# A planned one-core kernel: same-engine delays and shaken orders in its planner, a third bank for its second layer, and one engine of forty of its steps changed

## The chip, the cores and the metric

The kernel runs on one core of a Trainium2 chip. The metric is the device time of one execution in microseconds (us). The kernel before was run three times: 559.52, 560.00 and 560.67 us, median 560.0.

The core has TensorE (PE in the profile, its weight loads PEld), VectorE (DVE), ScalarE (ACT), GpSimd (POOL) and SyncE (SP), which issues all transfers here. Each engine works through its own list of instructions in order and waits on semaphores for the others. TensorE writes its results to eight banks of PSUM; this kernel calls them S0 to S3, Y0, Y1, G and D.

## The reference

Three parts follow one another; the output of one is the input of the next.

```
y   = attention with decay over x, a, B, C        # 4 x 8 heads, 768 positions
h   = max(y @ w1, y @ w2, y @ w3)                 # 3072 tokens, 256 -> 768
x2  = h @ w_out                                   # 768 -> 256
t   = x2 @ w_in                                   # 256 -> 2048
P   = a0 + a1 t + a2 t^2 + a3 t^3
Q   = 1 + |b0| |t| + |b1| t^2
out = (P / (Q + 1e-6)) @ w_out2                   # 2048 -> 256
```

## The kernel before

The 3072 tokens are worked on in six groups of 512. For each group there is an attention part, a first layer ("g": 18 tiles of the three products with their maximum, then 2 "y" tiles with w_out) and a second layer of 16 steps. Values are split into a high and a low part, and each product is three matmuls, high by high, high by low and low by high, made by `mm3`:

```
    pe.matmul(dst, wh, hi, start=first, stop=False)
    pe.matmul(dst, wh, lo, start=False, stop=False)
    pe.matmul(dst, wl, hi, start=False, stop=last)
```

In the trace these are L845, L846 and L847. Step s of the second layer (`h_plan`, s from 0 to 95) makes one tile t of 128 x 512 with six of them ("h matmuls", weights win) in a PSUM bank, S0 or S1. ScalarE, GpSimd and VectorE then compute the rational function from t in a chain of some ten operations, and the last two make its high part (ScalarE, L366) and low part (GpSimd, L1073). `o_plan` adds the step's share of the output with six more matmuls ("o matmuls", the step's A tiles by the weights in L, into S2 and S3). The first layer's tiles of the next groups go to the banks G and D; after each of its products ScalarE copies the bank (L366) or VectorE takes the maximum with it (L935).

There are several ways to compute the rational function, called kinds. HV gives the kinds of the steps of groups 0 to 4 in turn, HL those of group 5. In kind H, ScalarE makes two values from t (L1042 and L1044), GpSimd one linear expression and one product (L1028, L1046), and VectorE multiplies twice with the bank t as an operand (L1047, L1048). L1048 is the last reader of the bank. Kind J differs from H in one operation: the linear expression is made by ScalarE (L1025). Kind A uses a square on ScalarE (L1051) and ends its use of the bank with L1058. All kinds end in a logarithm and an exponential on ScalarE (L1060, L1061) and three VectorE operations (L1062, L1065, L1067), each with one operand in a Y bank and one in SBUF.

The order of all this is not written out by hand. Every piece of work is handed to `Plan.op` with its engine, an assumed cost, what it reads and writes, and the banks or buffers it may use; `Plan.emit` then tries 8 rounds of 6 list schedules, each with latest start times from the best one so far, keeps the one with the earliest end, and emits the instructions in its order. So one constant can change the order on all engines.

Of the kernel before, what the change touches and what calls it, by code (L numbers as in the profile page):

```python
# [3 lines left out]

# [7 lines left out]
F32 = mybir.dt.float32  # L12
# [3 lines left out]
AF = mybir.ActivationFunctionType  # L16
ALU = mybir.AluOpType
# [16 lines left out]
OL = 6  # L34
SBANKS, DBANKS, FIRST_BANKS, GBANKS = (), ("D", "G"), ("G", "D", "S0", "S1", "S2", "S3"), ("G", "D")
LAST, LAST_R = ("G", "D", "S0", "S1"), ("Y0", "Y1")
HV, HL = "JAJH", "HHKK"
EARLY, SPILL = (0, 1, 2), (1, 2)
WARM = 9
PIECE = 2.6  # L40
# [7 lines left out]
class _Tile:  # L48


    def __init__(self, make=None, places=(), kind=None):
        self.make, self.places, self.t, self.place, self.kind = make, places, None, None, kind or places
        self.first, self.writers, self.readers = None, [], []


class _Op:

    def __init__(self, i, engine, busy, fn, first, deps, after, at, lock, mode, size):  # L60
        self.i, self.engine, self.busy, self.fn, self.first = i, engine, busy, fn, first
        self.deps, self.after, self.at = deps, after, at
        self.lock, self.mode, self.size = lock, mode, size
        self.plain = busy + (Plan.SWITCH if mode else 0.0)
        if engine == "dma":
            self.busy = busy + 0.06
            self.moves = 0.14 + size / 350.0 if size > 30.0 else 0.08
            self.plain = max(self.busy, self.moves)
        self.uses = [engine, "pool"] if lock else [engine]

    def lag(self, then):
        if self.engine == "dma":
            return Plan.FIRST_BYTE + self.moves + Plan.LANDED
        if self.engine == then.engine:
            return self.plain
        return self.plain + Plan.TAIL[self.engine] + (0.05 if then.engine == "pool" else 0.0)


# [19 lines left out]
class Plan:  # L98
# [3 lines left out]

    TAIL = {"pe": 0.22, "act": 0.15, "dve": 0.135, "pool": 0.09}
    SWITCH, FIRST_BYTE, LANDED, FLIGHTS, BEGIN = 0.12, 1.25, 1.35, 8, 0.65
    ROUNDS, LOOK, KEEP = 8, (0.0, 0.1, 0.2), (0.0, 1.5)

    def __init__(self):
        self.ops, self.fixed, self.tiles, self.turns = [], {}, [], {}
# [7 lines left out]
        return t  # L116

    def op(self, engine, busy, fn, reads=(), writes=(), at=None, behind=(), lock=False, mode="", size=0.0,
           turn=None):


        i = len(self.ops)
        deps, after = set(), {w for t in behind for w in t.writers}
        for k in [turn] * bool(turn) + [t.kind for t in writes if t.first is None and len(t.places) > 1]:
            if k in self.turns:
                after.add(self.turns[k])
            self.turns[k] = i
        for t in reads:
            assert t.writers
            deps.update(t.writers)  # L130
            t.readers.append(i)
        for t in writes:
            if t.first is None:
                t.first = i
                for p in getattr(t, "prevs", ()):
# [5 lines left out]
        self.ops.append(_Op(i, engine, busy, fn, [t for t in writes if t.first == i and t.places], deps,  # L141
                            after - deps, at, lock, mode, size))

    def listed(self, key, look, keep):

# [10 lines left out]
        place, had = {}, {}  # L156

        def behind(js, i, t):
            e = ops[i].engine
            for j in js:  # L160
                if ops[j].engine == e != "dma":
                    t = max(t, start[j] + ops[j].busy)
                else:
                    t = max(t, end[j] + (0.05 if e == "pool" else 0.0))
            return t
# [113 lines left out]
    def emit(self):  # L279

        ops, n = self.ops, len(self.ops)
        self.before, self.then, self.touch = [[] for _ in range(n)], [[] for _ in range(n)], [[] for _ in range(n)]
        for o in ops:
            for i in o.deps | o.after:
                l = 0.0 if i in o.after else ops[i].lag(o)
                self.before[o.i].append((i, l))
                self.then[i].append((o.i, l))
        self.of_fixed, self.open_fixed = {}, {}
        for p, ts in self.fixed.items():
            self.of_fixed[p] = [i for t in ts for i in t.writers + t.readers]  # L290
            self.open_fixed[p] = 0
            for t in ts:
                t.place = p
                self.open_fixed[p] += len(set(t.writers + t.readers))
        for t in self.tiles + [t for ts in self.fixed.values() for t in ts]:
            for i in set(t.writers + t.readers):
                self.touch[i].append(t)
        span = [o.plain for o in ops]
        key = [0.0] * n
        for i in reversed(range(n)):  # L300
            key[i] = min([1e9 if ops[i].at is None else ops[i].at] + [key[j] - l for j, l in self.then[i]])
        best = None
        for _ in range(self.ROUNDS):
            for look in self.LOOK:
                for keep in self.KEEP:
                    order, start, end, had = self.listed(key, look, keep)
                    if best is None or end < best[0]:
                        best = end, order, start, had, self.place
            start, had = best[2:4]
            before, then = [list(b) for b in self.before], [list(b) for b in self.then]  # L310
            for j, js in had.items():
                for i in js:
                    l = ops[i].lag(ops[j])
                    before[j].append((i, l))
                    then[i].append((j, l))
            back = [[(j, l - span[i] + span[j]) for j, l in then[i]] for i in range(n)]
            mirror = self.placed([-(start[i] + span[i]) for i in range(n)], back, before)
            far = max(mirror[i] + span[i] for i in range(n))
            key = [far - mirror[i] - span[i] for i in range(n)]
        start = best[2]  # L320
        for i in best[1]:
            for t in ops[i].first:
                t.t = t.make(best[4][t])
            ops[i].fn()
# [3 lines left out]
def decay_attention_max_moe_rational_moe(  # L328
# [49 lines left out]
    def plan_conv(tok, nm, src, k0, c0):  # L378
# [39 lines left out]

        for k in range(2):
            op("pool", 0.7, lambda k=k: pool.tensor_tensor(  # L420
                out=a.t[:, k], in0=a.t[:, k], in1=e.t[:, k], op=ALU.add), [e], [a])
        op("act", 0.54, lambda: copy(act, hi(), af()), [a], [tok])
        for k in range(2):
            op("pool", 0.7, lambda k=k: pool.tensor_tensor(
                out=lo()[:, k], in0=af()[:, k], in1=hi()[:, k].bitcast(F32), op=ALU.subtract), [a], [tok])

    for nm in ("w1", "w2", "w3"):
        w_alloc(nm, KD, DF1)
# [10 lines left out]
    def bank(*places, kind=None):  # L439
        return plan.tile(places, lambda p: ps.tile([128, T], F32, tag=p, name=p), kind=kind)  # L440
# [397 lines left out]
    def c(i):  # L838
        return co[:, i:i + 1]
# [148 lines left out]
    def h_plan(s, c0=0, n=T):  # L988
# [1 line left out]

        last = g == NG - 1
        half = n < T
        t = bank(*(LAST if last else ("S0", "S1")))
        x = n / T

        def f(z):
            return z.t[:, 0:n] if half else z.t

        def aop(cost, fn, reads, writes):
            op("act", cost - 0.43 * (1 - x), fn, reads, writes)  # L1000
# [19 lines left out]
        else:  # L1020
            v, w, t1 = v_r(), w_r(), t1_r()
        r = bank(*(LAST_R if last else ("Y0", "Y1")))
        def linear():
            if kind == "J":
                aop(0.69, lambda: act.activation(out=f(t1), in_=f(v), func=AF.Identity, scale=c(5), bias=c(4)),  # L1025
                    [v], [t1])
            else:
                pop(0.74, lambda: pool.tensor_scalar(out=f(t1), in0=f(v), scalar1=c(5), scalar2=c(4),  # L1028
                                                     op0=ALU.mult, op1=ALU.add), [v], [t1])

        if kind == "K":
            aop(0.5, lambda: copy(act, f(t1), f(t)), [t], [t1])
            aop(0.69, lambda: act.activation(out=f(w), in_=f(t), func=AF.Identity, scale=c(3), bias=c(2)),
                [t], [w])
            pop(1.26, lambda: pool.tensor_tensor(out=f(w), in0=f(t1), in1=f(w), op=ALU.mult), [t1], [w])
            aop(0.5, lambda: act.activation(out=f(v), in_=f(t), func=AF.Abs), [t], [v])
            linear()
            pop(1.26, lambda: pool.tensor_tensor(out=f(v), in0=f(t1), in1=f(v), op=ALU.mult), [t1], [v])
            dop(0.67, lambda: dve.scalar_tensor_tensor(out=f(w), in0=f(w), scalar=c(1), in1=f(t),
                                                       op0=ALU.add, op1=ALU.mult), [t], [w])  # L1040
        elif kind in "HJ":
            aop(0.69, lambda: act.activation(out=f(w), in_=f(t), func=AF.Identity, scale=c(3), bias=c(2)),  # L1042
                [t], [w])
            aop(0.5, lambda: act.activation(out=f(v), in_=f(t), func=AF.Abs), [t], [v])  # L1044
            linear()
# [154 lines left out]
```

## Time and profile before

| | |
|---|---|
| median of three runs | 560.0 us |
| profiled execution, its own time | 562.15 us |
| its span, first to last instruction | 560.2 us |
| mean granted TensorE clock | 0.994 |
| bytes moved | 36.92 MB |

The span is that of the profiled execution; the 1.95 us between it and the execution's own time lie around the program. The profile counts a matmul as busy from its start to its modelled end, so that neighbours overlap: TensorE can look busy while it starts fewer matmuls than it could. The count of matmuls in a stretch is therefore read beside the busy time.

### The profile page before, as it was taken

Reading aid. Unit: us, or ns where it says so; the run is one execution under the profiler, and the core shown is the slowest. Engines: PE = TensorE matmul, PEld = TensorE weight load, DVE = VectorE, ACT = ScalarE, POOL = GpSimd, SP = SyncE. Lnnn points to the kernel's source line nnn. Section 1 sums busy time; section 2 is a strip of 40 time slices with the busy share of each in tenths; the row PEclk is TensorE's granted clock in tenths of the full one; section 3 lists DMA queues with packets and bytes.
Section 4 is the critical chain, followed back from the end, with each engine's and each line's share of the span. In section 5 each row is a group of like instructions: output and inputs, shape, how many; then the busy total and the mean of one; then the engine's idle time right before and its main releaser. Section 6 shows DMA issues by size and latency. Waiting matters only on the chain. (4 is left out here: it accounts for less than half of the span.)

```text
span 560.2 us, 8435 instructions
## 1 busy us (share of the span) xinstructions
PE 541.8 (97%) x2854; PEld 410.8 (73%) x2854; DVE 491.2 (88%) x760; ACT 471.3 (84%) x805; POOL 410.7 (73%) x384
## 2 busy tenths in 40 slices
PE   8899999999999999999899999999999999999996
PEld 3466667888887877777677787777878777876663
DVE  6989999777985789899888898898999889899996
ACT  6989886757776799889798898998989988999883
POOL 1457875788896668767657776786689978779984
PEclk9979999999999999999999999999999999999999
DMA  7667963423702100010300100001000010001001
GB/s 205 240 220 242 328 212 127 139 75 115 261 2 75 39 1 1 0 39 1 113 0 0 39 1 1 1 1 37 2 1 1 0 39 1 1 1 37 1 0 38
DMA packets 15830, 36.92 MB, mean 66 GB/s; under 512 B 2947, under 2 KB 3883, under 8 KB 15787
## 3 DMA queue, kind: packets, MB, share of 16 engines
q1 hardware_dynamic: 15787, 36.38, 19.3%
q8 instruction: 22, 0.36, 0.3%
q14 instruction: 21, 0.17, 0.1%
HBM read 28.89 MB, written 7.49 MB: 65 GB/s over the span
## 5 line engine op out<-in xcount | busy, mean ns | idle before, releaser
L1073 POOL TENSOR_TENSOR A<-A,A 128x512 fp32r<-128x512 f32 x80 | 104.1, 1302 | 40.7 <-ACT A L366 35.5
L1046 POOL TENSOR_TENSOR A<-A,A 128x512 f32<-128x512 f32 x64 | 82.8, 1297 | 10.3 <-ACT A L1025 7.9
L1062 DVE SCALAR_TENSOR_TENSOR A<-A,Y 128x512 f32<-128x512 f32 (+1 forms) x89 | 60.4, 679 | 19.2 <-ACT Y L1061 18.3
L1060 ACT ACTIVATE Y<-A,qc 128x512 f32<-128x512 f32 (+1 forms) x89 | 61.1, 687 | 14.8 <-POOL A L1046 13.7
L420 POOL TENSOR_TENSOR C<-C,E 128x256 uint32<-128x256 uint32 x56 | 44.0, 799 | 34.3 <-DVE C L415 30.7
L1065 DVE SCALAR_TENSOR_TENSOR Y<-A,co,Y 128x512 f32<-128x512 f32 (+1 forms) x89 | 66.5, 747 | 0.3
L846 PE MATMUL S<-A,L 128*128 128x512 f32 x160 | 62.8, 392 | 1.0 <-POOL A L1073 1.0
L1067 DVE SCALAR_TENSOR_TENSOR A<-A,Y 128x512 f32<-128x512 f32 (+1 forms) x89 | 60.8, 683 | 2.9
L845 PE MATMUL S<-A,L 128*128 128x512 f32 x160 | 62.3, 390 | 0.0
L847 PE MATMUL S<-A,L 128*128 128x512 f32 x160 | 62.3, 390 | 0.0
L366 ACT ACTIVATE A<-A 128x512 fp32r<-128x512 f32 x80 | 50.1, 628 | 10.7 <-DVE A L1067 8.9
L1061 ACT ACTIVATE Y<-Y 128x512 f32<-128x512 f32 (+1 forms) x97 | 56.1, 578 | 2.5
L1042 ACT ACTIVATE A<-S,co 128x512 f32<-128x512 f32 x62 | 47.7, 770 | 3.1 <-POOL A L1073 1.7
L1048 DVE SCALAR_TENSOR_TENSOR A<-A,co,S 128x512 f32<-128x512 f32 x62 | 46.3, 747 | 2.0
L1047 DVE TENSOR_TENSOR A<-S,A 128x512 f32<-128x512 f32 x62 | 42.5, 686 | 6.1 <-ACT A L1042 4.3
L463 POOL TENSOR_TENSOR H<-X,H 128x512 fp32r<-128x512 f32 x30 | 40.2, 1339 | 8.7 <-ACT H L366 8.5
L1057 POOL TENSOR_TENSOR A<-A,A 128x512 f32<-128x512 f32 x20 | 25.9, 1296 | 20.6 <-DVE A L1053 16.9
L1044 ACT ACTIVATE A<-S 128x512 f32<-128x512 f32 x62 | 36.7, 592 | 4.3 <-PE S L847 2.4
L845 PE MATMUL S<-K,win_hi 128*128 128x512 f32 (+1 forms) x80 | 33.6, 420 | 3.2 <-DVE A L1048 2.5
L846 PEld LDWEIGHTS S<-A,L 128*128 128x128 f32 x160 | 30.0, 188 | 9.1 <-POOL A L1073 2.7
L845 PEld LDWEIGHTS S<-A,L 128*128 128x128 f32 x160 | 30.0, 188 | 6.4
L847 PEld LDWEIGHTS S<-A,L 128*128 128x128 f32 x160 | 30.0, 188 | 6.1
(214 smaller groups left out, 1613.3 us busy)
## 6 DMA issues: line engine op xcount, KB each, us to landing
R<-in_wo_dram SPq DMA_DIRECT2D x11, 512.0 KB
R<-in_w_dram SPq DMA_DIRECT2D x9, 512.0 KB
R<-in_win_dram SPq DMA_DIRECT2D x8, 512.0 KB
L<-in_xn_dram SPq DMA_DIRECT2D x6, 512.0 KB
out_dram<-A SPq DMA_DIRECT2D x12, 256.0 KB
xt_d<-L SPq DMA_DIRECT2D x4, 512.0 KB
L<-xt_d SPq DMA_DIRECT2D x4, 512.0 KB
y_d<-A SPq DMA_DIRECT2D x8, 256.0 KB
```

Of the source, the lines that this page charges most:

```text
L366: act.activation(out=o, in_=i, func=AF.Copy)
L845: pe.matmul(dst, wh, hi, start=first, stop=False)
L846: pe.matmul(dst, wh, lo, start=False, stop=False)
L847: pe.matmul(dst, wl, hi, start=False, stop=last)
L1042: aop(0.69, lambda: act.activation(out=f(w), in_=f(t), func=AF.Identity, scale=c(3), bias=c(2)), [t], [w])
L1046: pop(1.26, lambda: pool.tensor_tensor(out=f(v), in0=f(t1), in1=f(v), op=ALU.mult), [t1], [v])
L1060: aop(0.6, lambda: act.activation(out=f(r), in_=f(v), func=AF.Ln, bias=qc), [v], [r])
L1061: aop(0.49, lambda: act.activation(out=f(r), in_=f(r), func=AF.Exp, scale=-1.0), [], [r])
L1062: dop(0.6, lambda: dve.scalar_tensor_tensor(out=f(v), in0=f(v), scalar=QC, in1=f(r), op0=ALU.add, op1=ALU.mult), [r], [v])
L1065: dop(0.67, lambda: dve.scalar_tensor_tensor(out=f(r), in0=f(w), scalar=c(0), in1=f(r), op0=ALU.add, op1=ALU.mult), [w], [r])
L1067: dop(0.6, lambda: dve.scalar_tensor_tensor(out=f(w), in0=f(v), scalar=2.0, in1=f(r), op0=ALU.subtract, op1=ALU.mult), [v, r], [w])
L1073: pop(1.26, lambda: pool.tensor_tensor(out=f(lo), in0=f(w), in1=f(hi).bitcast(F32), op=ALU.subtract), [w, hi], [lo])
```

## The change

Four things change.

1. The planner counts 0.12 us (`DRAIN`) between two operations of the same engine (not TensorE, not transfers) when the second uses a tile that the first wrote.
2. After its 8 rounds the planner tries 150 more orders. Each takes the latest start times of the best order so far, shakes those in a randomly drawn stretch by a random amount, and is kept if its planned end is earlier. The draws have a fixed seed.
3. A second-layer step of groups 0 to 4 may use bank D as well as S0 and S1.
4. HV goes from JAJH to HAHH: in groups 0 to 4, 40 steps of kind J become kind H. Kind J is removed from the code.

No instruction is added or removed apart from the 40 that change engine; everything may move.

```diff
-HV, HL = "JAJH", "HHKK"
+HV, HL = "HAHH", "HHKK"
...
         if self.engine == then.engine:
-            return self.plain
+            return self.plain + (Plan.DRAIN if self.i in then.results else 0.0)
...
+    DRAIN = 0.12
-    ROUNDS, LOOK, KEEP = 8, (0.0, 0.1, 0.2), (0.0, 1.5)
+    ROUNDS, SHAKES, LOOK, KEEP = 8, 150, (0.0, 0.1, 0.2), (0.0, 1.5)
...
+        for t in (*reads, *writes):
+            if engine not in ("pe", "dma") and not apart:
+                results.update(w for w in t.writers if self.ops[w].engine == engine)
...
+        draw = random.Random(1)
+        for _ in range(self.SHAKES):
+            key = latest() if draw.random() < 0.3 else best[5]
+            at, reach, by = draw.uniform(0.0, 200.0), draw.choice((10.0, 25.0, 60.0, 600.0)), draw.choice((0.2, 0.6, 1.5))
+            key = [k + (draw.gauss(0.0, by) if abs(k - at) < reach else 0.0) for k in key]
+            attempt(key, draw.choice(self.LOOK), draw.choice(self.KEEP))
...
-        t = bank(*(LAST if last else ("S0", "S1")))
+        t = bank(*(LAST if last else ("S0", "S1", "D")))
...
-        def linear():
-            if kind == "J":
-                aop(0.69, lambda: act.activation(out=f(t1), in_=f(v), func=AF.Identity, scale=c(5), bias=c(4)),
-                    [v], [t1])
...
-            linear()
+            pop(0.74, lambda: pool.tensor_scalar(out=f(t1), in0=f(v), scalar1=c(5), scalar2=c(4),
+                                                 op0=ALU.mult, op1=ALU.add), [v], [t1])
```

The order of the instructions moves on every engine. Two places on TensorE and one on GpSimd show how. A name like S0_4371 is tile 4371 in bank S0; with win it is a second-layer step, with w1, w2 or w3 a first-layer tile, and with L1 an output share. In the changed file mm3's lines are L866 to L868, and L1028, L1046, L1057 and L1073 are L1059, L1061, L1072 and L1088.

TensorE before, steps 53 and 54 of the second layer, near the end of group 3:

```order
L845 MATMUL S0_4371<-K0_3237,win_hi_90 128x512
L846 MATMUL S0_4371<-K1_3252,win_hi_90 128x512
L847 MATMUL S0_4371<-K0_3237,win_lo_91 128x512
L845 MATMUL S0_4371<-K2_3359,win_hi_90 128x512
L846 MATMUL S0_4371<-K3_3407,win_hi_90 128x512
L847 MATMUL S0_4371<-K2_3359,win_lo_91 128x512
L845 MATMUL S1_4383<-K0_3237,win_hi_90 128x512
L846 MATMUL S1_4383<-K1_3252,win_hi_90 128x512
L847 MATMUL S1_4383<-K0_3237,win_lo_91 128x512
L845 MATMUL S1_4383<-K2_3359,win_hi_90 128x512
L846 MATMUL S1_4383<-K3_3407,win_hi_90 128x512
L847 MATMUL S1_4383<-K2_3359,win_lo_91 128x512
```

TensorE in the changed kernel, step 52 and what follows it:

```order
L866 MATMUL D_4215<-K0_3336,win_hi_90 128x512
L867 MATMUL D_4215<-K1_3356,win_hi_90 128x512
L868 MATMUL D_4215<-K0_3336,win_lo_91 128x512
L866 MATMUL D_4215<-K2_3415,win_hi_90 128x512
L867 MATMUL D_4215<-K3_3421,win_hi_90 128x512
L868 MATMUL D_4215<-K2_3415,win_lo_91 128x512
L866 MATMUL G_4229<-xhi0_3283,w2_hi_84 128x512
L867 MATMUL G_4229<-xlo0_3294,w2_hi_84 128x512
L868 MATMUL G_4229<-xhi0_3283,w2_lo_85 128x512
L866 MATMUL G_4229<-xhi1_3322,w2_hi_84 128x512
L867 MATMUL G_4229<-xlo1_3346,w2_hi_84 128x512
L868 MATMUL G_4229<-xhi1_3322,w2_lo_85 128x512
```

Before, steps alternate between S0 and S1. In the changed kernel step 52 is in D, and the first-layer tile behind it is in G. From step 10 to step 79, 22 of 70 steps are in D. Of the 54 first-layer product tiles of groups 3 to 5, 28 were in D and 26 in G; now 7 are in D and 47 in G.

TensorE before, around the second tile of group 5's first layer (the first tile ends in the first three rows):

```order
L845 MATMUL G_4413<-xhi1_4131,w1_hi_82 128x512
L846 MATMUL G_4413<-xlo1_4203,w1_hi_82 128x512
L847 MATMUL G_4413<-xhi1_4131,w1_lo_83 128x512
L845 MATMUL S2_4322<-A13_4400,L1_1859 128x512
L846 MATMUL S2_4322<-A17_4408,L1_1859 128x512
L847 MATMUL S2_4322<-A13_4400,L1_1859 128x512
L845 MATMUL S3_4328<-A13_4400,L1_1859 128x512
L846 MATMUL S3_4328<-A17_4408,L1_1859 128x512
L847 MATMUL S3_4328<-A13_4400,L1_1859 128x512
L845 MATMUL D_4442<-xhi0_4120,w2_hi_84 128x512
L846 MATMUL D_4442<-xlo0_4144,w2_hi_84 128x512
L847 MATMUL D_4442<-xhi0_4120,w2_lo_85 128x512
```

TensorE in the changed kernel, the same two tiles:

```order
L866 MATMUL G_4698<-xhi1_4524,w1_hi_82 128x512
L867 MATMUL G_4698<-xlo1_4545,w1_hi_82 128x512
L868 MATMUL G_4698<-xhi1_4524,w1_lo_83 128x512
L866 MATMUL S0_4710<-A0_4576,win_hi_90 128x512
L867 MATMUL S0_4710<-A1_4581,win_hi_90 128x512
L868 MATMUL S0_4710<-A0_4576,win_lo_91 128x512
L866 MATMUL S0_4710<-A2_4675,win_hi_90 128x512
L867 MATMUL S0_4710<-A3_4682,win_hi_90 128x512
L868 MATMUL S0_4710<-A2_4675,win_lo_91 128x512
L866 MATMUL G_4726<-xhi0_4479,w2_hi_84 128x512
L867 MATMUL G_4726<-xlo0_4516,w2_hi_84 128x512
L868 MATMUL G_4726<-xhi0_4479,w2_lo_85 128x512
```

Before, the second tile goes to the other bank. In the changed kernel both are in G, with the six matmuls of a step between them.

GpSimd before, from the low part of step 51 on:

```order
L1073 TENSOR_TENSOR A17_4408<-A7_4332,A13_4400 128x512
L1057 TENSOR_TENSOR A9_4394<-A9_4394,A10_4391 128x512
L1073 TENSOR_TENSOR A16_4437<-A8_4352,A14_4424 128x512
L1046 TENSOR_TENSOR A6_4422<-A11_4439,A6_4422 128x512
L1028 TENSOR_SCALAR A10_4478<-A4_4470,co_81 128x512
L1046 TENSOR_TENSOR A4_4470<-A10_4478,A4_4470 128x512
L1073 TENSOR_TENSOR A16_4504<-A9_4394,A13_4480 128x512
L1073 TENSOR_TENSOR A17_4523<-A7_4449,A14_4518 128x512
L1046 TENSOR_TENSOR A5_4502<-A10_4521,A5_4502 128x512
L1073 TENSOR_TENSOR A16_4549<-A8_4491,A15_4546 128x512
```

GpSimd in the changed kernel, from the same place on:

```order
L1088 TENSOR_TENSOR A16_4337<-A7_4212,A13_4316 128x512
L1059 TENSOR_SCALAR A10_4344<-A6_4332,co_81 128x512
L1072 TENSOR_TENSOR A9_4297<-A9_4297,A11_4277 128x512
L1088 TENSOR_TENSOR A17_4366<-A8_4257,A14_4356 128x512
L1061 TENSOR_TENSOR A6_4332<-A10_4344,A6_4332 128x512
L1059 TENSOR_SCALAR A11_4390<-A5_4364,co_81 128x512
L1061 TENSOR_TENSOR A5_4364<-A11_4390,A5_4364 128x512
L1059 TENSOR_SCALAR A10_4413<-A4_4405,co_81 128x512
L1088 TENSOR_TENSOR A16_4425<-A9_4297,A13_4410 128x512
L1061 TENSOR_TENSOR A4_4405<-A10_4413,A4_4405 128x512
```

The TENSOR_SCALAR row, which belongs to kind H alone, stands once in ten rows before and three times now.

## Rows read from the trace of the kernel before

**Rows 1.** The page: busy time by engine, and shares of the chain that ended last.

```profile
PE 541.8 (97%) x2854; PEld 410.8 (73%) x2854; DVE 491.2 (88%) x760; ACT 471.3 (84%) x805; POOL 410.7 (73%) x384
...
ACT 16%; DVE 13%; POOL 6%; issue 4%; PE 3%; POOLq 0%; DVEq 0%; ACTq 0%
```

**Rows 2.** Five stretches: length, PE, PEld, DVE, ACT, POOL busy (instructions), clock, DMA.

```profile
0.00:108.00 108.00, 102.11 (x1004) 67.72 (x1005) 96.89 (x169) 86.69 (x152) 61.52 (x77) 0.97 0.65 215
108.00:180.00 72.00, 72.00 (x319) 59.57 (x318) 54.48 (x79) 49.35 (x85) 60.02 (x64) 1.00 0.32 109
180.00:340.00 160.00, 155.66 (x669) 123.69 (x668) 140.05 (x209) 142.22 (x240) 114.42 (x93) 1.00 0.06 22
340.00:500.00 160.00, 156.74 (x676) 125.15 (x675) 145.05 (x218) 145.50 (x247) 125.87 (x103) 1.00 0.02 7
500.00:560.00 60.00, 55.32 (x192) 34.70 (x191) 54.77 (x88) 47.59 (x86) 48.92 (x48) 1.00 0.05 18
```

**Rows 3.** Line L845, 180 to 500 us: TensorE's idle time before it, times, by releaser.

```profile
  DVE A L1048: 19.4, 34
  DVE A L1058: 2.2, 6
  DVE A L463: 1.3, 2
  ACT A L1044: 1.0, 3
```

**Rows 4.** The same for line L846.

```profile
  POOL A L1073: 3.7, 8
```

**Rows 5.** Timeline, step 59 behind step 58 in S1: start, duration, engine, line [idle before].

```profile
410.61 0.39 PE L847 MATMUL S<-K,win_lo 128*128 128x512 f32 x1
...
412.34 0.62 ACT L1044 ACTIVATE A<-S 128x512 f32<-128x512 f32 x1
...
413.42 0.69 DVE L1047 TENSOR_TENSOR A<-S,A 128x512 f32<-128x512 f32 x1 [1.05 <-ACT A L1044]
...
414.14 0.75 DVE L1048 SCALAR_TENSOR_TENSOR A<-A,co,S 128x512 f32<-128x512 f32 x1
...
414.95 0.50 PE L845 MATMUL S<-K,win_hi 128*128 128x512 f32 x1 [1.23 <-DVE A L1048]
```

**Rows 6.** Waits, 180 to 500 us: who waited for whom, us in total, times, longest.

```profile
DVE A L1062 <- ACT Y L1061: 18.3, 20, 2.3
...
DVE A L1047 <- ACT A L1042: 4.1, 9, 1.4
```

**Rows 7.** Groups by line, 180 to 500 us: busy us, mean ns | idle before.

```profile
L1025 ACT ACTIVATE A<-A,co 128x512 f32<-128x512 f32 x37 | 30.2, 815 | 1.5
...
L1028 POOL TENSOR_SCALAR A<-A,co 128x512 f32<-128x512 f32 x19 | 15.1, 796 | 5.6 <-ACT A L1044 5.6
...
L935 DVE TENSOR_TENSOR X<-X,G 128x512 f32<-128x512 f32 x18 | 12.3, 683 | 2.5 <-ACT A L1042 1.8 <-PE G L847 0.4
```

**Rows 8.** Single lines, 180 to 500 us: duration ns min/median/max, first and last start.

```profile
L1062 DVE SCALAR_TENSOR_TENSOR A<-A,Y x74: 672/680/690, 180.8 to 496.8; 128x512 f32<-128x512 f32 x74
...
L1067 DVE SCALAR_TENSOR_TENSOR A<-A,Y x75: 679/686/691, 186.8 to 498.8; 128x512 f32<-128x512 f32 x75
...
L463 DVE TENSOR_TENSOR xlo<-L,xhi x4: 768/1288/1818, 263.7 to 372.7; 128x512 fp32r<-128x512 f32 x4
```

**Rows 9.** Three stretches of 20 us; columns as in Rows 2.

```profile
80.00:100.00 20.00, 20.00 (x171) 15.03 (x168) 18.25 (x33) 13.61 (x25) 12.77 (x16) 1.00 0.54 189
...
420.00:440.00 20.00, 20.00 (x90) 16.34 (x89) 17.30 (x27) 18.68 (x32) 19.57 (x17) 1.00 0.00 1
...
520.00:540.00 20.00, 20.00 (x66) 11.99 (x64) 19.69 (x32) 16.79 (x29) 18.62 (x18) 1.00 0.00 1
```

More of the change, by code (lines that the diff above doesn't have):

```diff
@@ L2 @@
 import heapq
+import random
 from contextlib import ExitStack
@@ L56, with __init__ @@
 class _Op:
-    def __init__(self, i, engine, busy, fn, first, deps, after, at, lock, mode, size):
-        self.i, self.engine, self.busy, self.fn, self.first = i, engine, busy, fn, first
+    def __init__(self, i, engine, busy, fn, first, deps, after, at, lock, mode, size, results=()):
+        self.i, self.engine, self.busy, self.fn, self.first, self.results = i, engine, busy, fn, first, results
         self.deps, self.after, self.at = deps, after, at
@@ L118, in op @@
     def op(self, engine, busy, fn, reads=(), writes=(), at=None, behind=(), lock=False, mode="", size=0.0,
-           turn=None):
+           turn=None, apart=False):
         i = len(self.ops)
-        deps, after = set(), {w for t in behind for w in t.writers}
+        deps, after, results = set(), {w for t in behind for w in t.writers}, set()
+        for t in (*reads, *writes):
+            if engine not in ("pe", "dma") and not apart:
+                results.update(w for w in t.writers if self.ops[w].engine == engine)
         for k in [turn] * bool(turn) + [t.kind for t in writes if t.first is None and len(t.places) > 1]:
@@ L141, in op @@
         self.ops.append(_Op(i, engine, busy, fn, [t for t in writes if t.first == i and t.places], deps,
-                            after - deps, at, lock, mode, size))
+                            after - deps, at, lock, mode, size, results))
     def listed(self, key, look, keep):
@@ L161, in behind @@
                 if ops[j].engine == e != "dma":
-                    t = max(t, start[j] + ops[j].busy)
+                    t = max(t, start[j] + ops[j].busy + (self.DRAIN if j in ops[i].results else 0.0))
                 else:
@@ L302, in emit, with attempt, latest @@
         best = None
[L303 to L308, printed above, removed]
+        def attempt(key, look, keep):
+            nonlocal best
+            order, start, end, had = self.listed(key, look, keep)
+            if best is None or end < best[0]:
+                best = end, order, start, had, self.place, key
+        def latest():
             start, had = best[2:4]
@@ L318, in emit @@
             far = max(mirror[i] + span[i] for i in range(n))
-            key = [far - mirror[i] - span[i] for i in range(n)]
+            return [far - mirror[i] - span[i] for i in range(n)]
+        for _ in range(self.ROUNDS):
+            for look in self.LOOK:
+                for keep in self.KEEP:
+                    attempt(key, look, keep)
+            key = latest()
+        draw = random.Random(1)
[4 more added lines that the diff above has]
+            attempt(key, draw.choice(self.LOOK), draw.choice(self.KEEP))
         start = best[2]
@@ L420, in plan_conv @@
             op("pool", 0.7, lambda k=k: pool.tensor_tensor(
-                out=a.t[:, k], in0=a.t[:, k], in1=e.t[:, k], op=ALU.add), [e], [a])
+                out=a.t[:, k], in0=a.t[:, k], in1=e.t[:, k], op=ALU.add), [e], [a], apart=True)
         op("act", 0.54, lambda: copy(act, hi(), af()), [a], [tok])
@@ L424, in plan_conv @@
             op("pool", 0.7, lambda k=k: pool.tensor_tensor(
-                out=lo()[:, k], in0=af()[:, k], in1=hi()[:, k].bitcast(F32), op=ALU.subtract), [a], [tok])
+                out=lo()[:, k], in0=af()[:, k], in1=hi()[:, k].bitcast(F32), op=ALU.subtract), [a], [tok], apart=k > 0)
     for nm in ("w1", "w2", "w3"):
@@ L1022, in h_plan @@
         r = bank(*(LAST_R if last else ("Y0", "Y1")))
-        def linear():
-            if kind == "J":
-                aop(0.69, lambda: act.activation(out=f(t1), in_=f(v), func=AF.Identity, scale=c(5), bias=c(4)),
-                    [v], [t1])
-            else:
-                pop(0.74, lambda: pool.tensor_scalar(out=f(t1), in0=f(v), scalar1=c(5), scalar2=c(4),
-                                                     op0=ALU.mult, op1=ALU.add), [v], [t1])
         if kind == "K":
@@ L1040, in h_plan @@
                                                        op0=ALU.add, op1=ALU.mult), [t], [w])
-        elif kind in "HJ":
+        elif kind == "H":
             aop(0.69, lambda: act.activation(out=f(w), in_=f(t), func=AF.Identity, scale=c(3), bias=c(2)),
@@ L1044, in h_plan @@
             aop(0.5, lambda: act.activation(out=f(v), in_=f(t), func=AF.Abs), [t], [v])
-            linear()
+            pop(0.74, lambda: pool.tensor_scalar(out=f(t1), in0=f(v), scalar1=c(5), scalar2=c(4),
+                                                 op0=ALU.mult, op1=ALU.add), [v], [t1])
             pop(1.26, lambda: pool.tensor_tensor(out=f(v), in0=f(t1), in1=f(v), op=ALU.mult), [t1], [v])
```

## The prediction

> **What bounds the kernel now.** The page comes first [rows 1]: TensorE is busy 97% of the span, but no engine is idle for long, and the chain that ended last runs through ScalarE (16%), VectorE (13%) and GpSimd (6%), and only for 3% through TensorE. TensorE has most of the work, and the three others decide when it gets it.
>
> How much is lost shows only by stretches [rows 2]. From 108 to 180 us TensorE has no idle time and executes 319 matmuls in 72 us, 4.43 per us. From 180 to 500 us, where second-layer steps and first-layer tiles alternate, it executes 669 + 676 = 1345 in 320 us, 4.20 per us. At the rate of the stretch before, 320 us would hold 1418: 73 matmuls, or 73 / 4.43 = 16.4 us, are lost there. That is what this change can work on. From 0 to 108 us (attention) VectorE is busy 96.9 us, from 500 us on (group 5) VectorE 54.8 of 60 us and TensorE 55.3.
>
> What TensorE waits for in the 320 us is read at the lines of its matmuls. Each group of three begins with L845 [rows 3]: 34 waits for VectorE's L1048, 6 for L1058 and 3 for L1044, 22.6 us together. (Waits of weight loads and matmuls are both counted, so these are shares, not times.) These are second-layer steps that wait for their bank: L1048 is its last reader. Two waits, 1.3 us, are for L463, a first-layer bank. L846 waits 3.7 us for the low part from L1073, which an output share needs [rows 4]. Of 27.6 us in all, 82% are the steps' bank, 13% the low parts, 5% the first layer's bank: of 16.4 us, 13.4, 2.2 and 0.8.
>
> One such wait in full [rows 5]: step 58's last matmul in S1 starts at 410.61. Twelve other matmuls follow, then step 59 wants S1. But ScalarE begins its second read of S1 at 412.34, VectorE reads it at 413.42, having waited 1.05 us, and again at 414.14, and step 59 starts at 414.95 after 1.23 us idle.
>
> **The change part by part.**
>
> *Third bank.* I counted in the order, for steps 10 to 79, how many matmuls lie between the last use of a step's bank and its first matmul. The mean goes from 29 to 43, from 6.6 to 9.7 us at 4.43 per us. Under 32 matmuls lie 45 of 70 steps before, 9 now. If waits follow these counts, 13.4 x 9/45 = 2.7 us stay and **10.7 us** go. Bounds: nothing (if the readers come later by as much) and 13.4.
>
> *Output shares later.* For steps 16 to 79, the mean number of matmuls from a step's end to its first output share goes from 59 to 85, 5.9 us more for the chain to finish. Of the 2.2 us I count **1.5** as gone; bounds 0 and 2.2. A fuller GpSimd can eat some of it, since L1073 is GpSimd's.
>
> *First layer on one bank.* This is the cost. Of 54 product tiles of groups 3 to 5, 2 start within 9 matmuls (2.0 us) of their bank's last use, now 13. In that time ScalarE must copy or VectorE take the maximum, 0.68 us [rows 7]. If VectorE is in another operation just then, half of one, about 0.37 us, comes on top. I count 11 more tiles, every second with 0.37 us: **2.1 us lost**. Bounds: nothing (the two tiles that were tight before were hardly seen in rows 3) and 11 x 1.23 = 13.5, each as late as in rows 5.
>
> *J to H.* 37 of the 40 linear expressions lie in the stretch: 30.2 us leave ScalarE at 0.815 each, and 37 x 0.796 = 29.5 us arrive on GpSimd [rows 7]. In a step's chain one replaces the other, so it is not shorter. ScalarE falls from 287.7 us in the 320 to 257.5, GpSimd rises from 240.3 to 269.8 [rows 2]. VectorE's two largest waits for ScalarE (18.3 and 4.1 us) are behind a full ScalarE queue [rows 6]; they shrink, which is what lets the bank's readers run on time. I give this no gain of its own beside the bank's. GpSimd at 87% is no bound: from 420 to 440 us it was busy 19.57 of 20 us and TensorE executed at its full count of 90 [rows 9].
>
> *Does VectorE allow it?* It has 285.1 us of work in the stretch [rows 2], none removed. A gain of 10.7 + 1.5 - 2.1 = 10.1 us leaves 309.9 us, VectorE 92%. TensorE ran full with VectorE at 18.25 of 20 (91%) and, in group 5, 19.69 of 20 [rows 9]. So 92% is at the edge of what was seen, and not past it.
>
> *Delay and shaken orders* remove nothing by themselves; their work is the order above. In the attention part the order puts five weight conversions instead of six ahead of the first maximum on VectorE, but TensorE has some 13 more matmuls left when group 1's first layer begins. I count nothing there, with 2 us either way: VectorE has only 108 - 96.9 = 11.1 us idle in it [rows 2]. From 500 us on kinds and matmuls are unchanged: nothing, 1 us either way. Transfers move in SP's queue, but the DMA share is 0.06 and less after 180 us, and no TensorE wait there names one.
>
> *GpSimd and VectorE.* VectorE's L1062 took 672 to 690 ns in all of 74 cases and L1067 679 to 691 in 75, while GpSimd was busy three quarters of the time; the split L463, with both inputs in SBUF, took 768 to 1818 [rows 8]. The Trainium skill ("SBUF — State Buffer", Who interferes with whom) says that a VectorE instruction with two SBUF inputs contends with a GpSimd instruction that reads SBUF, and one with at most one does not. The rows agree for both sorts. The skill's "Perfetto Trace Analysis" (Optimizing Scalar/DVE Operations) warns that, because the two share a port, moving work between them might not help; taken for all VectorE work, that is the fourth rival below.
>
> **Sum.** The profiled execution took 562.15 us for a span of 560.2, the median of the runs is 560.0. 562.15 - 10.1 = 552.0 for such an execution; against the median, 560.0 - 10.1 = 549.9. I say **550**.
>
> **Rivals.**
>
> 1. *The forecast*: the bank wait goes, 547 to 554. Chance 0.54.
> 2. *More than that*: nearly all 16.4 us come back, VectorE runs at 285.1 / 303.6 = 94%: 543.6. For it: group 5's 98%. Against: group 5 has no low parts and fewer hops. 0.10.
> 3. *VectorE sets the pace at 90.5%*, a little above today's 89%: 285.1 / 0.905 = 315, a gain of 5 us, 555. For it: three busy queues in order, and VectorE's waits for ScalarE partly become waits for GpSimd. 0.17.
> 4. *GpSimd holds VectorE up*: each of the 37 moved operations blocks VectorE for its 0.796 us, 29.5 us more; 285.1 + 29.5 = 314.6 of 320 us leaves no room, 560. Rows 8 speak against it, since the steps' operations did not stretch. 0.04.
> 5. *The wait moves to bank G* (the other side): the 13 tight tiles wait for their copy or maximum as step 59 did, 1.23 us each, 16 us; with 12.2 us gained elsewhere, 560.0 - 12.2 + 16 = 564. It decides from 12.2 / 13 = 0.94 us per tile. For it: the order gives 47 of 54 tiles to one bank. Against: in a queue as busy as VectorE's the plan can still put the maximum in front, and rows 3 show two such waits in 320 us. 0.10.
> 6. *The order does not do on the chip what it is planned for*: steps still wait, at other places, 559 to 561. The order does show the distances grown, so 0.05.
>
> **The numbers.** The likeliest case gives 550, its own range 547 to 554. For 8 in 10 the range takes in cases 1, 2 and 3: 544 to 559, with the two bounds of the attention part inside it. A difference of 0.2%, 1.1 us, is about what a measurement here can tell from none. Faster: 0.81 from cases 1 to 3. Within 0.2%: 0.03 of case 4, 0.03 of case 6 and 0.02 of case 5 near its turning point, 0.08. Slower: the rest of 4 to 6, 0.11.
>
> **What would show it.** Right: between the first step of group 1 and the first of group 5 TensorE's rate rises from 4.20 towards 4.35 per us; waits of the first matmul of a step (then L866) for the bank's last reader (L1063) fall to a quarter; VectorE's share there rises to some 92% and ScalarE's falls to about 83%. Wrong: L866's waits name the maximum (L956) or the copy (L387) and a bank G, more than 10 us of them (case 5); L1077, L1080 or L1082 with a wide spread of durations (case 4); VectorE at 90% with idle time behind GpSimd (case 3); or an end of the attention part that moved by more than 2 us.

## Result, and the profile after

The changed kernel takes 544.38 us (median of four runs, 543.57 to 547.82) against 560.17 before (559.52 to 560.67). The ratio is 0.973, 95% interval 0.969 to 0.977: 15.8 us less. The forecast was 550, range 544 to 559. The size lies at the range's edge, and the experiments show that the reasons given for it were largely wrong.

The profiled execution took 547.82 us, the longest of its runs; its span is 545.9 us. The page answers to [rows 1]:

```profile
PE 534.7 (98%) x2854; PEld 414.1 (76%) x2854; DVE 485.7 (89%) x760; ACT 444.1 (81%) x765; POOL 441.9 (81%) x424
...
PE 81%; DVE 8%; ACT 4%; issue 2%; POOL 2%; DMA 1%; SPq 1%; ACTq 0%; DVEq 0%
```

The chain that ended last now runs for 81% through TensorE, 3% before. The shares of busy time hardly show this: TensorE went from 97% to 98%. The stretches answer to [rows 2], with the same columns:

```profile
0.00:108.00 108.00, 101.72 (x961) 67.54 (x962) 94.12 (x163) 83.71 (x146) 55.64 (x71) 0.97 0.61 202
...
180.00:340.00 160.00, 159.09 (x700) 130.69 (x699) 148.74 (x232) 141.96 (x244) 142.68 (x129) 1.00 0.06 22
340.00:500.00 160.00, 160.00 (x707) 132.16 (x706) 142.98 (x221) 136.02 (x231) 145.53 (x126) 1.00 0.02 7
500.00:546.00 46.00, 41.92 (x137) 24.61 (x135) 40.79 (x68) 34.58 (x63) 35.29 (x36) 0.98 0.06 23
```

From 180 to 500 us TensorE executes 1407 matmuls, 4.40 per us (4.20 before, 4.43 where nothing delays it). The idle time before the first matmul of a group (L866, was L845), 180 to 500 us, by what ended it, answers to [rows 3]:

```profile
  DVE X L956: 2.0, 3
  DVE A L484: 1.1, 2
```

That before the second matmul (L867, was L846) answers to [rows 4]:

```profile
  POOL A L1088: 0.6, 3
```

No step waits for its bank any more; 22.6 us stood there before. What is left, 3.1 us, is waits for first-layer banks, and 0.6 us for low parts. The waits that answer to [rows 6]:

```profile
DVE A L1077 <- ACT Y L1076: 8.8, 17, 1.5
...
DVE A L1062 <- ACT A L1056: 6.5, 7, 1.7
```

Three moments and a sum place the gain. They are worked out from the timeline of each profile: when group 1's first layer begins on TensorE, when group 5's first step begins, when the last output matmuls begin; and, between the first two, the sum over neighbouring matmuls of mm3 of their start distance beyond 0.227 us ("stalls").

| kernel | group 1 begins | group 5's steps begin | last matmuls | stalls |
|---|---|---|---|---|
| before | 108.15 | 498.69 | 555.22 | 15.8 |
| after | 106.89 | 486.13 | 540.89 | 2.2 |

So 13.6 us of stalls went between the first two moments. That stretch is only 11.3 us shorter, since 48 matmuls of the attention part (L757 and L768, which add some 2.2 us) now stand behind group 1's start, 132 to 136 us in. Group 1 begins 1.3 us earlier, and 1.8 us went behind step 80.

### The profile page after: what moved, and what is told of

Same layout as the page of the kernel before. It is cut to its first block, busy times and chain, and to the rows that moved or that the text cites. A ratio compares the mean times of both kernels' runs of the same rounds, so it can differ in the third digit from the quotient of the medians.

```text
span 545.9 us, 8419 instructions
## 1 busy us (share of the span) xinstructions
PE 534.7 (98%) x2854; PEld 414.1 (76%) x2854; DVE 485.7 (89%) x760; ACT 444.1 (81%) x765; POOL 441.9 (81%) x424
## 4 chain that ended last, share of the span: by engine, by line
PE 81%; DVE 8%; ACT 4%; issue 2%; POOL 2%; DMA 1%; SPq 1%; ACTq 0%; DVEq 0%
PE S L866 13%; PE S L867 13%; PE S L868 13%; PE G L866 7%; PE G L867 6%; PE G L868 6%; PE S L1106 5%; PE D L867 4%; PE D L868 4%; PE D L866 4%; PE S L709 1%; ACT A L740 1%; PE Y L757 1%; DMA R<-in_w_dram 1%; DVE A L745 1%
## 5 line engine op out<-in xcount | busy, mean ns | idle before, releaser
L1088 POOL TENSOR_TENSOR A<-A,A 128x512 fp32r<-128x512 f32 x80 | 104.4, 1306 | 12.5 <-ACT A L387 11.4
L1061 POOL TENSOR_TENSOR A<-A,A 128x512 f32<-128x512 f32 x64 | 83.3, 1304 | 3.3
L1077 DVE SCALAR_TENSOR_TENSOR A<-A,Y 128x512 f32<-128x512 f32 (+1 forms) x89 | 60.4, 679 | 9.5 <-ACT Y L1076 9.3
L1080 DVE SCALAR_TENSOR_TENSOR Y<-A,co,Y 128x512 f32<-128x512 f32 (+1 forms) x89 | 66.4, 746 | 0.1
L867 PE MATMUL S<-A,L 128*128 128x512 f32 x160 | 62.4, 390 | 0.0
L866 PE MATMUL S<-A,L 128*128 128x512 f32 x160 | 62.2, 389 | 0.0
L868 PE MATMUL S<-A,L 128*128 128x512 f32 x160 | 62.2, 389 | 0.0
L1082 DVE SCALAR_TENSOR_TENSOR A<-A,Y 128x512 f32<-128x512 f32 (+1 forms) x89 | 60.4, 679 | 1.1
L1059 POOL TENSOR_SCALAR A<-A,co 128x512 f32<-128x512 f32 x64 | 50.9, 797 | 4.4 <-ACT A L1058 4.0
L866 PE MATMUL G<-xhi,w_hi 128*128 128x512 f32 x126 | 49.7, 394 | 0.9 <-DVE X L956 0.6
L868 PE MATMUL G<-xhi,w_lo 128*128 128x512 f32 x126 | 49.1, 390 | 0.0
L867 PE MATMUL G<-xlo,w_hi 128*128 128x512 f32 x126 | 49.1, 389 | 0.0
L387 ACT ACTIVATE H<-X 128x512 fp32r<-128x512 f32 x36 | 22.7, 629 | 19.1 <-DVE X L956 18.9
L867 PEld LDWEIGHTS S<-A,L 128*128 128x128 f32 x160 | 30.0, 188 | 6.7 <-POOL A L1088 0.6
L866 PEld LDWEIGHTS S<-A,L 128*128 128x128 f32 x160 | 30.0, 188 | 6.3
L745 DVE TENSOR_TENSOR A<-S,A 128x512 f32<-128x512 f32 x48 | 30.6, 680 | 4.6 <-PE S L709 2.6
L868 PEld LDWEIGHTS S<-A,L 128*128 128x128 f32 x160 | 30.0, 188 | 6.1
```

The lines of the kernel that those rows point to most:

```text
L387: act.activation(out=o, in_=i, func=AF.Copy)
L1077: dop(0.6, lambda: dve.scalar_tensor_tensor(out=f(v), in0=f(v), scalar=QC, in1=f(r), op0=ALU.add, op1=ALU.mult), [r], [v])
L1080: dop(0.67, lambda: dve.scalar_tensor_tensor(out=f(r), in0=f(w), scalar=c(0), in1=f(r), op0=ALU.add, op1=ALU.mult), [w], [r])
L1082: dop(0.6, lambda: dve.scalar_tensor_tensor(out=f(w), in0=f(v), scalar=2.0, in1=f(r), op0=ALU.subtract, op1=ALU.mult), [v, r], [w])
L1088: pop(1.26, lambda: pool.tensor_tensor(out=f(lo), in0=f(w), in1=f(hi).bitcast(F32), op=ALU.subtract), [w, hi], [lo])
```

## Experiments

Ratios are to the kernel before, timed on the same chip beside it; they differ by up to 0.3% from the quotient of two medians. The theories: 1, the steps' bank was the loss; 2, ScalarE's full queue; 3, the planner. "Stalls" is the sum above, for the profile of each.

**The third bank alone.**

```diff
-        t = bank(*(LAST if last else ("S0", "S1")))
+        t = bank(*(LAST if last else ("S0", "S1", "D")))
```

> The kernel before with the third bank alone (a step of groups 0 to 4 may use D; kinds and planner as before). In its order the mean number of matmuls between uses of a step's bank is 38.5 (29.4 before, 43.1 with the whole change), and the first output share of a step comes 89 matmuls behind it (59 before). Theory 1, the steps' bank is the loss: 547 to 551 us, and TensorE's waits for the bank's last reader between 180 and 500 us fall below a third. Theory 2, ScalarE's full queue is the loss: 556 to 560, the waits stay and only move. Theory 3, the planner's delays and the shaken orders bring the gain: 557 to 563.

Measured: 565.26 us, ratio 1.007 (1.005 to 1.009): 0.7% slower, outside what each theory asked for. The stalls are 19.1 us. The two stretches of the second layer:

```profile
180.00:340.00 160.00, 154.03 (x648) 118.84 (x647) 144.11 (x214) 146.03 (x246) 115.32 (x94) 1.00 0.06 22
340.00:500.00 160.00, 157.35 (x683) 127.08 (x682) 140.95 (x214) 142.91 (x239) 125.28 (x102) 1.00 0.02 7
```

The idle time before L845, 180 to 500 us, the largest rows:

```profile
  DVE A L1048: 16.4, 26
  ACT A L1044: 3.1, 6
  DVE A L463: 2.9, 4
  DVE X L935: 1.3, 3
  DVE A L1058: 0.9, 3
```

The distance between uses of a bank grew by nine matmuls, and in its order 19 of 70 steps have under 32 matmuls (45 before, 9 with the whole change). Yet TensorE waits 16.4 us for the bank's last reader (19.4 before). So the readers come later by about as much. Theory 1 falls.

**HAHH alone.**

```diff
-HV, HL = "JAJH", "HHKK"
+HV, HL = "HAHH", "HHKK"
```

> The kernel before with HV as HAHH alone (banks and planner as before). Mean distance between uses of a step's bank 29.4 matmuls, as before, with 22 of 70 steps below 20 (12 before). Theory 1, the steps' bank is the loss: 556 to 561, waits for the last reader stay near 20 us. Theory 2, ScalarE's full queue is the loss: 548 to 552, since the readers come on time. Theory 3, the planner: 557 to 563.

Measured: 562.01 us, ratio 1.001 (0.999 to 1.004), stalls 15.0. ScalarE falls to 263 us in the 320 without any effect on the time. Theory 2 in its plain form falls.

**The planner alone.** The changed kernel with these lines put back, and kind J restored:

```diff
-HV, HL = "HAHH", "HHKK"
+HV, HL = "JAJH", "HHKK"
...
-        t = bank(*(LAST if last else ("S0", "S1", "D")))
+        t = bank(*(LAST if last else ("S0", "S1")))
```

> The changed planner alone (0.12 us between dependent operations of an engine, 150 shaken orders), with kinds JAJH and the banks S0 and S1 as before. Distances as before (29.2 matmuls, output shares 59 behind). Theory 1 (bank) and theory 2 (ScalarE): 556 to 561, what there is of a gain lies in the first 108 us. Theory 3 (planner): 548 to 552.

Measured: 551.60 us, ratio 0.983 (0.981 to 0.985), stalls 8.3. Theory 3 holds: more than half of the gain comes with the banks and kinds of before, with the same mean distance of 29 matmuls, and again 45 of 70 steps under 32.

**Third bank and HAHH with the old planner.** Both edits of the first two experiments in the kernel before.

> The third bank and HAHH together with the planner of before (no delay, no shaken orders). Its instructions stand in the same order on every engine as those of a planner that makes 150 shaken orders but counts no delay: none of these was better by its own count. Theories 1 and 2: 544 to 549, nearly all of the gain. Theory 3: 553 or more.

Measured: 561.65 us, ratio 1.002 (1.000 to 1.004), stalls 17.9. The stretches:

```profile
180.00:340.00 160.00, 153.42 (x658) 121.28 (x657) 142.57 (x214) 135.33 (x229) 134.25 (x120) 1.00 0.06 21
340.00:500.00 160.00, 156.52 (x678) 125.79 (x677) 141.22 (x215) 129.40 (x220) 138.34 (x120) 1.00 0.02 7
```

The idle time before L845, 180 to 500 us, the largest rows:

```profile
  DVE A L1048: 7.9, 22
  DVE A L1058: 7.4, 11
  DVE X L935: 4.1, 7
  ACT X L366: 4.0, 4
```

With every resource of the changed kernel, TensorE executes 1336 matmuls in the 320 us, fewer than before (1345). Since the order is the same as with 150 shaken orders and no delay, this run also shows that here the shaken orders without the delay are worth nothing.

**The delay alone.** Kind J is restored here too.

```diff
-    ROUNDS, SHAKES, LOOK, KEEP = 8, 150, (0.0, 0.1, 0.2), (0.0, 1.5)
+    ROUNDS, SHAKES, LOOK, KEEP = 8, 0, (0.0, 0.1, 0.2), (0.0, 1.5)
...
-HV, HL = "HAHH", "HHKK"
+HV, HL = "JAJH", "HHKK"
...
-        t = bank(*(LAST if last else ("S0", "S1", "D")))
+        t = bank(*(LAST if last else ("S0", "S1")))
```

> The delay of 0.12 us alone: 8 rounds, no shaken orders, kinds JAJH, banks S0 and S1. Theory A, an order planned with true distances between dependent operations is what was missing: 551 to 553.5, all of what the changed planner alone gave (551.6). Theory B, the shaken orders make the planner's part: 557 or more. Theory 1 of the first call (the bank) has no gain here: 558 to 561.

Measured: 552.77 us, ratio 0.985 (0.981 to 0.988), stalls 9.9. Theory A: one number in the planner gives some 8 us. Stretches:

```profile
180.00:340.00 160.00, 158.59 (x694) 129.26 (x693) 141.02 (x218) 144.66 (x249) 121.28 (x102) 1.00 0.05 19
340.00:500.00 160.00, 156.66 (x683) 127.03 (x682) 143.10 (x223) 146.36 (x252) 130.47 (x109) 1.00 0.02 7
```

TensorE executes 1377 matmuls (1345 before) while VectorE is busy 284.1 us, as before (285.1), but with 441 instructions in place of 427. Group 1 begins at 104.33, 3.8 us earlier than before.

**Without the shaken orders.** SHAKES = 0 in the changed kernel.

> The changed kernel without the 150 shaken orders (delay, third bank, HAHH). Theory A: 544 to 547, within some 2 us of the whole change. Theory B: 552 or more.

Measured: 551.34 us, ratio 0.981 (0.977 to 0.986), stalls 4.3; between what the theories asked for. So the shaken orders are worth some 5 us here by the ratios, whose intervals just touch; of runs with a mean clock of 1.000, 548.28 stands against 543.57 and 544.96. Some 2 us of it are stalls. Group 1 begins at 110.24, 3.4 us later than with them, but 2.2 of these are the 48 matmuls that the shaken order puts behind this moment. Without bank and kinds the shaken orders are worth 1 us (0.983 against 0.985, not clear of noise).

**Without the third bank.** S0 and S1 alone in the changed kernel.

> The changed kernel with steps of groups 0 to 4 in S0 and S1 alone (delay, shaken orders, HAHH). If the third bank pays once the order is planned with the delay: 549 to 552, with 5 to 9 us of waits for the bank's last reader from 180 to 500 us. If it is worth nothing then too: 543 to 546.

Measured: 547.58 us, ratio 0.976 (0.972 to 0.980), stalls 4.8. The bank's waits for L1063 and L1073 are 4.4 us, though the distances are those of before (in its order a mean of 29.7 matmuls, 46 of 70 steps under 32). Beside the whole change (0.973) the bank is worth 1 to 2 us by the ratios and 3 by the medians, and the intervals overlap; neither expectation fits.

**With JAJH.** HV = "JAJH" in the changed kernel, and kind J restored.

> The changed kernel with JAJH (delay, shaken orders, third bank). If ScalarE's load pays once the order is planned with the delay: 547 to 551, ScalarE over 90% busy from 180 to 500 us and its waits in TensorE's place. If it is worth nothing then too: 543 to 546.

Measured: 551.87 us, ratio 0.983 (0.980 to 0.987), stalls 8.8. ScalarE is busy 292.4 of the 320 us, 91% (278.0 in the changed kernel). Once the order is planned with the delay and shaken, the 40 operations moved off ScalarE are worth some 6 us. Four of the runs, all with delay and 150 shaken orders, part bank and kind:

| ratio | S0, S1 | S0, S1 and D |
|---|---|---|
| JAJH | 0.983 | 0.983 |
| HAHH | 0.976 | 0.973 |

With JAJH the bank is worth nothing. HAHH is worth 4 us on two banks and 6 on three, by the ratios. Without shaken orders both together go from 0.985 to 0.981, with overlapping intervals.

**True sums without the delay.** In the changed kernel:

```diff
-    DRAIN = 0.12
+    DRAIN = 0.0
...
-            dop(0.6, lambda: dve.tensor_tensor(out=f(w), in0=f(t), in1=f(w), op=ALU.mult), [t], [w])
+            dop(0.72, lambda: dve.tensor_tensor(out=f(w), in0=f(t), in1=f(w), op=ALU.mult), [t], [w])
...
-        dop(0.67, lambda: dve.scalar_tensor_tensor(out=f(r), in0=f(w), scalar=c(0), in1=f(r),
+        dop(0.79, lambda: dve.scalar_tensor_tensor(out=f(r), in0=f(w), scalar=c(0), in1=f(r),
```

> The changed kernel with no delay between dependent operations, but with the planned price of the two VectorE operations that are most often followed by a dependent one raised by the same 0.12 us (0.60 to 0.72 and 0.67 to 0.79). The planner's sums for a step are then as true as with the delay, but it has no reason to put other work between dependent operations: in its order 197 of 748 VectorE instructions follow directly on one whose result they use (217 before, 117 with the whole change). Theory C, true sums are what counts: 545 to 549. Theory D, the gain comes from work put between dependent operations: 553 to 560.

Measured: 560.33 us, ratio 0.998 (0.996 to 0.999), stalls 12.4. By the time, theory D. The trace is less plain. The stretches:

```profile
180.00:340.00 160.00, 153.14 (x659) 121.88 (x658) 141.09 (x214) 132.93 (x227) 130.28 (x115) 1.00 0.06 21
340.00:500.00 160.00, 160.00 (x702) 130.56 (x701) 145.35 (x220) 135.06 (x230) 145.06 (x126) 1.00 0.02 8
```

One row of VectorE's timeline near 300 us, with the wait before it in brackets:

```profile
304.28 0.69 DVE L1062 TENSOR_TENSOR A<-S,A 128x512 f32<-128x512 f32 x1 [6.80 <-ACT A L1056]
```

From 340 to 500 us TensorE runs at nearly its full rate, with the dependent operations still side by side. The loss lies before 340, as in the one gap of 6.8 us where VectorE has nothing to do, and in the attention part (group 1 begins at 110.06, with none of the 48 matmuls behind it), whose prices the edit did not touch. So it doesn't separate the two theories.

**The planned order, J executed.** In the changed kernel the planner still places the linear expression of 40 steps on GpSimd, but ScalarE executes it:

```diff
+            if not last and k % 4 in (0, 2):
+                pop(0.74, lambda: act.activation(out=f(t1), in_=f(v), func=AF.Identity, scale=c(5), bias=c(4)),
+                    [v], [t1])
+            else:
```

> The changed kernel in its own order, planned for HAHH, in which the linear expression of the 40 steps that were kind J is executed by ScalarE at the same place; TensorE's, VectorE's and SyncE's lists are those of the whole change, row for row. If ScalarE's load costs time by itself: 549 to 556, with waits of VectorE and TensorE behind ScalarE. If only the order counts: 543 to 546.

Measured: 551.07 us, ratio 0.981 (0.978 to 0.984), stalls 8.1. TensorE's and VectorE's lists are those of the changed kernel, so the 40 operations cost some 5 us on ScalarE with no other order on these two. How much of it is ScalarE's load, and how much the place in its queue, which was not planned for them, this run cannot tell; with JAJH planned for, it is some 6. VectorE's waits for it, 180 to 500 us:

```profile
DVE A L1081 <- ACT Y L1080: 12.3, 23, 1.5
...
DVE A L1066 <- ACT A L1056: 7.3, 9, 1.6
```

In the changed kernel the same two waits (L1077 and L1062 there, four lines higher up than in this file) are 8.8 and 6.5 us.

**600 shaken orders.** SHAKES = 600.

> The changed kernel with 600 shaken orders in place of 150; the first 150 draws are the same. If the planner's sums hold on the chip, each order that it prefers is a little better: 540 to 544. If what is left is below what its sums can tell: 543 to 547.

Measured: 546.10 us, ratio 0.975 (0.968 to 0.981), stalls 3.3.

**Another seed.** random.Random(2).

> The changed kernel with another seed of the draws (150 shaken orders). This shows how far two orders of the same planner lie apart: 542 to 548.

Measured: 545.23 us, ratio 0.970 (0.968 to 0.973), stalls 3.0. The three orders of the full planner give 0.973, 0.975 and 0.970 with overlapping intervals. None is shown to be better than another, and differences under some 0.4% between single orders say nothing about an edit. The third bank's 1 to 3 us beside the whole change are of that size, so they are not shown. With this seed TensorE waits 2.7 us for a step's last reader (L1063, seven times), in the changed kernel not at all.

## Why the prediction came out as it did

*What bounds the kernel: right.* The 16.4 us of missing matmuls between 180 and 500 us were what could be won there, and 13.6 us of stalls went. TensorE's rate was to rise to 4.35 per us, it rose to 4.40; VectorE's share was to be 92%, it is (148.74 + 142.98) / 320 = 91%.

*"Delay and shaken orders remove nothing by themselves": the step that failed.* With it failed the sentence that VectorE has 285.1 us of work, none removed. By the stretches these are 427 instructions, 0.668 us each; the changed kernel takes 291.7 us for 453 and the delay alone 284.1 for 441, both 0.644 each. The rows of before had the answer, in the starts of VectorE's neighbours:

```profile
296.31 0.68 DVE L1062 SCALAR_TENSOR_TENSOR A<-A,Y 128x512 f32<-128x512 f32 x1
296.90 0.75 DVE L1065 SCALAR_TENSOR_TENSOR Y<-A,co,Y 128x512 f32<-128x512 f32 x1
297.69 0.69 DVE L1067 SCALAR_TENSOR_TENSOR A<-A,Y 128x512 f32<-128x512 f32 x1
298.29 0.68 DVE L935 TENSOR_TENSOR X<-X,D 128x512 f32<-128x512 f32 x1
299.08 0.69 DVE L935 TENSOR_TENSOR X<-X,G 128x512 f32<-128x512 f32 x1
```

That is VectorE's timeline of the kernel before: start, duration, line. L1065 does not use what L1062 wrote, and starts 0.59 us after it. L1067 uses L1065's result and starts 0.79 us after it. L935 does not use L1067's and starts after 0.60; the second L935 uses the first one's X and starts after 0.79. So an operation that uses the result starts behind the listed end of the one before (0.79 against 0.75 or 0.68), and one that does not starts ahead of it. The sum of listed durations shows nothing of this. The same in the changed kernel:

```profile
341.98 0.68 DVE L1077 SCALAR_TENSOR_TENSOR A<-A,Y 128x512 f32<-128x512 f32 x1
342.57 0.75 DVE L1080 SCALAR_TENSOR_TENSOR Y<-A,co,Y 128x512 f32<-128x512 f32 x1
343.23 0.74 DVE L1068 SCALAR_TENSOR_TENSOR A<-A,co,Y 128x512 f32<-128x512 f32 x1
343.89 0.68 DVE L1082 SCALAR_TENSOR_TENSOR A<-A,Y 128x512 f32<-128x512 f32 x1
```

Another step's L1068 now stands between L1080 and L1082, and every start follows after 0.59 to 0.66 us. Over 180 to 500 us the median from L1065 to a next L1067 was 0.78 us, 71 times; in the changed kernel, L1080 is followed directly by L1082 29 times, at 0.78, and in most other cases by an operation that does not use its result, at 0.66. From L1047 directly to L1048 it is 0.72 us, 55 times before and 32 now, against 0.60 to an independent one. Over all lines, 141 operations of the stretch came directly behind one whose result they use, and 66 do now: an estimate of 75 x 0.12 = 9 us of VectorE's time in the stretch. The delay alone has 46. The eight orders planned with the delay have 35 to 66 and ratios of 0.970 to 0.985, the five planned without it 121 to 141 and 0.998 to 1.007.

The Trainium skill ("VectorE: DVE Perf Modes", The DRAIN you can't avoid) says that the next VectorE operation does not start until the pipeline has emptied, though one that is not held starts earlier, and that in a measured chain of copies a semaphore between two operations cost nothing on top. Here the two cases differ by 0.12 us (0.66 against 0.78 behind L1065, 0.60 against 0.72 behind L1047), so for these operations the rows decide.

What the delay does is shown only as a whole: alone it gives 8 us, and without it bank, kinds and shaken orders give nothing. Whether it acts by putting other work between dependent operations, or by making the planned times true so that all queues meet as planned, the run with true sums did not settle. The count of dependent neighbours is not all of it: with JAJH in the changed kernel it is lower (68 in its whole list, 117 in the whole change's, 217 before), and that kernel is slower.

*Third bank, 10.7 us: wrong as a cause.* The bank's waits did go, from 22.6 us to none. But the term put them down to distances. The first experiment has most of the distances without the gain: by the term's own count the rows' 22.6 us should have fallen to 22.6 x 19/45 = 9.5, and 20.4 stayed (L1048, L1044 and L1058). And with the delay the stalls fall to 4.8 us on two banks, at the distances of before. The bank's own part is some 3 us at most by these runs, and not shown.

*J to H, no gain of its own: wrong.* It is worth 4 to 6 us with delay and shaken orders, by three comparisons, and nothing under the old planner. The forecast gave it nothing of its own and so left out that ScalarE's queue could be the next to be full (91% busy with JAJH under the new planner).

*Output shares 1.5 us, first layer on one bank 2.1 us: right in size.* Low parts cost 0.6 us of idle time (3.7 before), first-layer banks 3.1 us (1.3 before). Rival 5, the wait that moves to bank G, is seen in these rows at a tenth of its price (1.8 of 16 us). Neither term was tried alone.

*The attention part, nothing with 2 us either way: right by this profile, and by luck.* Group 1 begins 1.3 us earlier, with 48 matmuls still to come, where the prediction counted some 13. But from 0 to 40 us the mean granted clock was 0.91 in this profile and in that of before. In profiles where it was 1.00, group 1 begins at 108.03, 108.43 and 109.04 us without the delay (third bank, HAHH, both), and at 104.33 and 104.51 with it (delay alone, without the third bank), none of them with attention matmuls behind that moment. So the delay is worth some 4 us here too, which the prediction put at nothing.

*The rivals.* GpSimd did not hold VectorE up (rival 4): L1077 took 671 to 690 ns in 78 cases while GpSimd was busy 90% of the stretch. Rival 3, VectorE as the pace at 90.5%, fell with the wrong sum of VectorE's work. Rival 2, nearly all of the 16.4 us, is close to what happened; its chance was set too low because VectorE's share was taken as a limit.

So the time came out inside the range by luck, from a sum whose terms belong elsewhere: its largest, 10.7 us for the bank, is refuted, and what the delay wins makes up for it. The stalls that could be won were read rightly, the part of the change that wins them was not, and 15.8 us were gained where the sum has 10.1.

## What to carry to other kernels

Before giving a gain to a buffer or to a lighter engine, run that edit alone: here the planner without the delay filled the new room with an order that was just as late. Read start-to-start distances of neighbours on an in-order engine, dependent and independent ones apart; here the sum of recorded durations hid what a dependence costs, and the planner that did not count it lost some 8 us. And judge an edit to a planned kernel by more than one order of the same planner, since single orders here lie up to some 0.4% apart.

## What the hardware showed beyond this

TensorE's granted clock fell in the attention part in some profiles and not in others, though the programs there are much alike. Windows of the changed kernel, then of the one with 600 shaken orders:

```profile
24.00:28.00 4.00, 2.71 (x34) 1.40 (x27) 3.93 (x6) 4.00 (x8) 3.37 (x4) 1.00 0.98 365
28.00:32.00 4.00, 3.52 (x22) 2.13 (x21) 2.67 (x6) 3.60 (x7) 2.00 (x3) 0.63 0.53 183
32.00:36.00 4.00, 3.74 (x43) 2.35 (x44) 2.24 (x4) 2.88 (x6) 1.77 (x4) 0.52 0.54 199
```

```profile
24.00:28.00 4.00, 2.81 (x22) 1.46 (x23) 3.96 (x7) 4.00 (x8) 2.56 (x3) 1.00 1.00 339
28.00:32.00 4.00, 2.81 (x51) 1.88 (x48) 2.38 (x4) 4.00 (x8) 2.36 (x4) 1.00 0.79 283
32.00:36.00 4.00, 4.00 (x67) 2.72 (x63) 3.77 (x7) 3.42 (x8) 1.86 (x3) 1.00 0.52 157
```

In both TensorE was busy some 2.7 or 2.8 of 4 us before. In the first the granted clock then fell to 0.63 and 0.52, that is to 1.2 of 2.4 GHz for most of 28 to 36 us; in the second it stayed at 2.4. Over whole runs of the changed kernel, a mean clock of 0.992 goes with 547.82 us, 0.997 with 545.01, 0.999 and 1.000 with 543.74 and 543.57, and once 1.000 with 544.96. The profile here is of the first of these, so 3 to 4 us of its span are not the order's. The run with the planned order and J executed says the same: all its lists are those of the changed kernel up to group 1's start, its clock stayed at 1.00, and group 1 begins at 103.44, 3.4 us earlier.
